# Blocks of 512 tokens: a new order of the first four attention groups and their loads, head transposes and g's low part moved forward

## The chip, the cores and the metric

The kernel runs on one core of one Trainium2 chip. The metric is the device time of one execution in microseconds; the median of several runs counts. A core has a matrix engine (TensorE, in the rows PE, its weight loads PEld), a vector engine (VectorE, DVE), an activation engine (ScalarE, ACT), GpSimd (POOL), and SyncE (SP), whose queue issues nearly all DMA transfers of this kernel. Each engine works through its own instructions in their order and waits on semaphores for the others.

## The reference

Three stages in float32, one after the other, on 3072 tokens (4 batches of 768) of 512 numbers (8 heads of 64):

```python
for c in range(nc):                       # chunks of 32 queries
    k_full = concat([mem_k, k[c_start-16 : c_end+8]])   # 8 memory keys, at most 56 others
    scores = scale * matmul(q_c, k_full.T)
    a = exp(scores - max(scores)); a = a / (sum(a) + 1e-9)
    out[c_start:c_end] = matmul(a, v_full)
x = out as (3072, 512)
h = x @ w_in                              # 512 x 2048, given as 64-bit floats
g = where(h > 0, h, exp(min(h, 0)) - 1)
x = g @ w_out                             # 2048 x 512
a = x @ w1; b = x @ w2                    # 512 x 1024 each
return ((a * b) @ w3) @ w_out2
```

## The kernel before

**Precision.** Each factor of a large product is split into a high and a low part (both in a 32-bit matmul type), and three products hi*hi, hi*lo, lo*hi are summed (`mm3`, lines 131 to 133). The weights of the middle stage lie in memory as 64-bit floats; each 128-wide piece (a job, 512 KB) is loaded by SP (`raw_cols` L147, `raw_rows` L155) and turned into two 32-bit parts by ScalarE and VectorE.

**The feed.** `Feed` runs these jobs as a pipeline: one call of `step` does the high part of job i-2 (ScalarE, L179), the low part of job i-3 (VectorE, L182), the merge of job i-1 and the rebase of job i (ScalarE, L166). A job that `by_act` selects gets one more ScalarE step (`top`, L188) and one merge on VectorE (`merge`, L192); another takes two VectorE steps (`shift` L170 and `low` L174). `load` issues the transfers of the jobs ahead, at most six beyond the one at hand. Jobs 0 to 31 alternate between columns of w_in and rows of w_out: 0, 1, 2 and 4 are w_in 0 to 3, 3 and 5 are w_out 0 and 1, 6 is w_in 4, and so on.

**Attention.** The tokens go in 24 groups of 128 (six to a batch). The steps of a group G: `load_qk` (SP: L296, L297), `load_v` (SP: L306, L310, L312; five or nine transfers), `at_first` for the first group of a batch (TensorE transposes of 8 keys and 8 memory keys, L326, copied by ScalarE to `front` and `memo`), `at_turn` (TensorE transposes of q and k, L333 and L335; six ScalarE copies), `at_scores` (L357), `at_max` (VectorE L374, L375; exponential on ScalarE L376), `at_sum` (VectorE L382 to L385), `at_norm` (L394), `at_flip` (a VectorE transpose, L405, which writes pT), `at_values` (TensorE L416), and `at_out`, which splits the result into the high part (ScalarE L127) and the low part (VectorE L128) of `xhl`, the input of the middle stage. Groups 1 and 2 have buffers and PSUM banks of their own (`pair`); group 0 and all from 3 on share one pair of banks (`banks`).

**Order of the work.** All is written out by hand; no scheduler changes it. Groups 0 to 3, which fill block 0, run in the order of the string `START`: a letter for a step and a number for the group (u first, t turn, s scores, m max, z sum, n norm, p flip, v values, o out, k load of q and k, w load of v), and `f` for one step of the feed. Behind it comes the middle stage, six blocks of 512 tokens with 16 feature tiles each. For a feature tile n: `mm_h` (12 products of x with w_in), the exponential on ScalarE (`elu_exp`, L582, L583), the max on VectorE (`elu_max`, L588), g's high part (`elu_hi`, ScalarE L592) and low part (`elu_lo`, VectorE L596), and `mm_x` (12 products of g with w_out, two tiles later). The other groups are dealt out between these: `pace` gives each step of `chain` a slot, two slots to a feature tile and eight to a group; `at_first` has -0.5, so it runs right behind the previous group's `at_out` at 7.2. In the first two tiles of a block (`first`) the function `x()` with `mm_x` and one `at_step` runs ahead of `mm_h`. The last stage is not touched by the change.

The lines of the loop in which g's low part stands:

```python
if first:
    x()
if n < NH:
    if j == 0:
        feed.until(due[f])
    mm_h(n)
...
if FF1 < n < NH:
    elu_lo(n - 1)
if not first:
    x()
```

## Time and profile before

| what | value |
|---|---|
| runs (us) | 1090.22, 1090.37, 1092.13; median 1090.37 |
| profiled execution (us) | 1091.64, its span 1089.9 |
| TensorE busy | 1039.5 us, 95% |
| VectorE busy | 569.1 us, 52% |
| ScalarE busy | 456.6 us, 42% |
| DMA | 199.17 MB, mean 183 GB/s |

The profile is one execution with the start and length of each instruction. Busy times are added per engine; an engine that is always busy sets the time, and where it is idle a row in square brackets says for how long and what ended the wait. In the rows an arrow `out<-in` names the tiles that an instruction writes and reads, and `x4` means that four of the same kind are merged in one row. A float32 matmul other than those of `mm3` shows as two records.

### The profile page before, as it was taken

The page shows a single profiled execution, that of the slowest core. Times are in us where ns is not written, and L with a number is a line of the kernel's source. Part 1 is how long each engine was busy: PE and PEld are TensorE (multiplying, and loading weights), DVE is VectorE, ACT ScalarE, POOL GpSimd, SP SyncE. Part 2 cuts the span into 40 slices and gives each one's busy share as a digit, 9 for nine tenths or more (in the row PEclk, how much of TensorE's full clock was granted, in tenths as well). Part 3 has the DMA queues.
Part 4 walks back from the last instruction along what each step waited for, and adds up shares of the span by engine and source line. Part 5 has one row for each costly group of instructions (what it writes and reads, how often), then busy time and mean ns, then how long its engine had stood idle before and what let it go on. Part 6 is the DMA issues. An engine that isn't in the chain of part 4 may idle for free.

```text
span 1089.9 us, 19197 instructions
## 1 busy us (share of the span) xinstructions
PE 1039.5 (95%) x7760; PEld 888.9 (82%) x7760; DVE 569.1 (52%) x993; ACT 456.6 (42%) x884; POOL 1.7 (0%) x16
## 2 busy tenths in 40 slices
PE   4489999999999999999999999999999999999998
PEld 3367887887888787878887888789999999999997
DVE  4678856656666565757654234144443544443333
ACT  3477756554555454545554333022232232222222
POOL 0000000000000000000000000000000000000000
PEclk9889999999999999999999999999999999999999
DMA  8777846755766575648544846455466466555521
GB/s 179 186 221 203 245 123 178 234 181 167 211 221 197 175 213 163 218 155 251 161 155 146 289 136 203 138 180 163 154 208 227 155 205 230 159 172 183 184 86 58
DMA packets 178340, 199.17 MB, mean 183 GB/s; under 512 B 101964, under 2 KB 142924, under 8 KB 178252
## 3 DMA queue, kind: packets, MB, share of 16 engines
q1 hardware_dynamic: 177212, 197.69, 58.6%
q8 instruction: 61, 1.00, 0.4%
q10 hardware_dynamic: 1040, 0.26, 0.1%
q14 instruction: 27, 0.22, 0.1%
HBM read 154.93 MB, written 42.99 MB: 182 GB/s over the span
## 4 chain that ended last, share of the span: by engine, by line
PE 91%; ACT 3%; DVE 2%; DMA 2%; SPq 1%; issue 0%; ACTq 0%; DVEq 0%
PE bank L131 20%; PE bank L132 19%; PE bank L133 19%; PE bank L710 7%; PE bank L711 7%; PE bank L709 7%; PE banks L416 2%; PE banks L133 2%; PE banks L132 2%; PE banks L131 2%; PE banks L357 1%; PE banks L333 1%; PE banks L335 1%; DMA vw<-in_v_dram 1%; PE banks L451 1%; DMA qn<-in_q_dram 1%
## 5 line engine op out<-in xcount | busy, mean ns | idle before, releaser
L131 PE MATMUL bank<-xhl,w 128*128 128x512 f32 x384 | 156.2, 407 | 1.0 <-ACT xhl L127 0.7
L132 PE MATMUL bank<-g,w 128*128 128x512 f32 x384 | 150.6, 392 | 3.6 <-DVE g L596 3.6
L131 PE MATMUL bank<-g,w 128*128 128x512 f32 x384 | 153.2, 399 | 0.0
L132 PE MATMUL bank<-xhl,w 128*128 128x512 f32 x384 | 152.0, 396 | 0.0
L133 PE MATMUL bank<-xhl,w 128*128 128x512 f32 x384 | 152.0, 396 | 0.0
L133 PE MATMUL bank<-g,w 128*128 128x512 f32 x384 | 150.1, 391 | 0.0
L582 ACT ACTIVATE eg<-bank 128x512 f32<-128x512 f32 x96 | 57.3, 597 | 121.2 <-PE bank L133 121.1
L588 DVE SCALAR_TENSOR_TENSOR eg<-eg,bank 128x512 f32<-128x512 f32 x96 | 65.6, 683 | 75.9 <-ACT eg L583 75.7
L483 DVE TENSOR_TENSOR e<-bank,e 128x384 f32<-128x384 f32 x64 | 35.7, 557 | 119.2 <-PE bank L711 119.2
L132 PEld LDWEIGHTS bank<-g,w 128*128 128x128 f32 x384 | 72.2, 188 | 19.5 <-DVE g L596 5.6
L131 PEld LDWEIGHTS bank<-xhl,w 128*128 128x128 f32 x384 | 73.3, 191 | 16.7 <-ACT xhl L127 0.9
L133 PEld LDWEIGHTS bank<-xhl,w 128*128 128x128 f32 x384 | 73.4, 191 | 15.9
L132 PEld LDWEIGHTS bank<-xhl,w 128*128 128x128 f32 x384 | 73.4, 191 | 14.8 <-DVE xhl L128 0.4
L131 PEld LDWEIGHTS bank<-g,w 128*128 128x128 f32 x384 | 72.2, 188 | 15.8 <-ACT g L592 0.2
L133 PEld LDWEIGHTS bank<-g,w 128*128 128x128 f32 x384 | 72.1, 188 | 15.1
L710 PE MATMUL bank<-xd,w 128*128 128x384 f32 x224 | 75.9, 339 | 0.0
L592 ACT CAST g<-eg 128x512 fp32r<-128x512 f32 x96 | 59.6, 621 | 35.4 <-DVE eg L588 35.1
L596 DVE TENSOR_TENSOR g<-eg,g 128x512 fp32r<-128x512 f32 x96 | 65.7, 684 | 14.8 <-ACT g L592 14.5
L483 DVE TENSOR_TENSOR e<-bank,eg 128x384 f32<-128x384 f32 x64 | 35.6, 557 | 58.8 <-PE bank L711 58.8
L711 PE MATMUL bank<-xd,w 128*128 128x384 f32 x192 | 64.8, 337 | 0.0
L709 PE MATMUL bank<-xd,w 128*128 128x384 f32 x192 | 64.2, 335 | 0.0
L583 ACT ACTIVATE eg<-eg 128x512 f32<-128x512 f32 x96 | 60.7, 632 | 3.1
(159 smaller groups left out, 1849.5 us busy)
## 6 DMA issues: line engine op xcount, KB each, us to landing
w<-wqd SPq DMA_DIRECT2D x96, 512.0 KB
raw<-in_moe_w_dram SPq DMA_DIRECT2D x32, 512.0 KB
w<-shd SPq DMA_DIRECT2D x30, 512.0 KB
wqd<-st SPq DMA_DIRECT2D x24, 512.0 KB
raw<-in_moe_w_out_dram SPq DMA_DIRECT2D x22, 512.0 KB
w3d<-st SPq DMA_DIRECT2D x16, 512.0 KB
w<-w3d SPq DMA_DIRECT2D x16, 512.0 KB
w<-wqd SPq DMA_DIRECT2D x32, 256.0 KB
```

Source lines behind the costliest of these rows:

```text
L131: mm(o, lhsT=w_hi, rhs=x_hi, start=start, stop=False)
L132: mm(o, lhsT=w_hi, rhs=x_lo, start=False, stop=False)
L133: mm(o, lhsT=w_lo, rhs=x_hi, start=False, stop=stop)
L483: nc.vector.tensor_tensor(out=o, in0=a, in1=b, op=op)
L582: nc.scalar.activation(e, h_t[n], AF.Relu, scale=-1.0)
L583: nc.scalar.activation(e, e, AF.Exp, scale=-1.0)
L588: nc.vector.scalar_tensor_tensor(out=e, in0=e, scalar=-1.0, in1=h_t.pop(n), op0=ALU.add, op1=ALU.max)
L592: nc.scalar.copy(g_t[n][:, 0, :], eg_t[n])
L596: nc.vector.tensor_tensor(out=g[:, 1, :], in0=eg_t.pop(n), in1=g[:, 0, :].bitcast(F32), op=ALU.subtract)
L709: mm(o, lhsT=args[0], rhs=args[2], start=start and i == 0, stop=False, skip_group_check=more)
L710: mm(o, lhsT=args[0], rhs=args[3], start=False, stop=False, skip_group_check=more)
L711: mm(o, lhsT=args[1], rhs=args[2], start=False, stop=i == 1, skip_group_check=more)
```

## The change

- `START` has a new order, and new words `l3`, `l4`, `l6`, which allow the feed to load so many jobs and issue those loads there. The feed's new field `cap` holds this limit: 2 ahead of the string, and all jobs behind it. The loads ahead of the string are q and k of groups 0, 1, 2, then v of group 0, then two weight jobs.
- `by_act` selects three of four later jobs in place of one of two.
- `at_first` of group 0 writes to another bank. From group 6 on it is called as `first_next` at slot 4.6 of the group before.
- `at_turn` copies `front` and `memo` first, and for groups 0 and 1 the copy of q goes to VectorE.
- A first ScalarE copy from the cleared `front` to `memo` is new.
- `elu_lo(n - 1)` stands ahead of `x()` in the first two tiles of a block, from the second tile of block 1 on.

```diff
@@ -69,7 +69,7 @@
     LATER = (11, 12, 13, 14, 15, 27, 28, 29, 30, 31)
     SHARED = {2: 24, 3: 25, 4: 26}
 
-    START = "u0 t0 k3 f s0 t1 f m0 s1 z0 n0 m1 p0 t2 v0 w3 s2 z1 n1 p1 m2 o0 t3 v1 s3 z2 n2 p2 f o1 v2 m3 f o2 z3 n3 p3 k4 v3 w4 f o3 f"
+    START = "u0 t0 w1 k3 l3 w2 l4 t1 s0 m0 s1 m1 t2 f z0 n0 p0 s2 f m2 v0 w3 l6 z1 n1 o0 p1 t3 f z2 n2 s3 v1 p2 m3 k4 f o1 v2 z3 n3 o2 p3 f v3 w4 f o3"
     SCALE = 1.0 / float(D) ** 0.5
     assert GQ == P and KEYS == 64 and KT == 4 and HP == 4 and DM == 512
 
@@ -206,15 +206,15 @@
 
 
         def __init__(self, jobs):
-            self.jobs, self.at, self.loaded = jobs, 0, 0
+            self.jobs, self.at, self.loaded, self.cap = jobs, 0, 0, 0
 
         def load(self, n):
-            while self.loaded < min(len(self.jobs), n):
+            while self.loaded < min(self.cap, n):
                 self.jobs[self.loaded].fetch()
                 self.loaded += 1
 
         def by_act(self, i):
-            return i < 6 or i % 2 == 1
+            return i < 6 or i % 4 != 2
 
         def do(self, i, *ops):
             if 0 <= i < len(self.jobs):
@@ -321,7 +321,7 @@
         if G % GPS:
             return
         n = RIGHT + NM
-        pk = bank(G, 1, n)
+        pk = bank(1 if G == 0 else G, 1, n)
         for hp in range(HP):
             nc.tensor.transpose(pk[:, hp, :], pair(head, hp), ident[:n, :n])
         nc.scalar.copy(front[:, :, 0, LEFT:FRONT], pk[:, :, 0:RIGHT])
@@ -334,13 +334,13 @@
         for hp in range(HP):
             nc.tensor.transpose(pk[:, hp, :], pair(kn, hp), ident)
         qT = at_tile(G, at_p, [P, HP, GQ], "qT", "qp")
-        nc.scalar.copy(qT, pq)
         kT = at_tile(G, at_p, [P, HP, NCG, KEYS], "kT", "ke")
         blocks = pk.rearrange("p a (c k) -> p a c k", k=CH)
+        nc.scalar.copy(kT[:, :, 0:1, 0:FRONT], front)
+        nc.scalar.copy(kT[:, :, :, WIN:KEYS], memo.to_broadcast([P, HP, NCG, NM]))
+        copy_on("v" if G < 2 else "a", qT, pq)
         nc.scalar.copy(kT[:, :, :, FRONT:WIN], blocks)
         nc.scalar.copy(kT[:, :, 1:NCG, 0:FRONT], blocks[:, :, 0:NCG - 1, CH - FRONT:CH])
-        nc.scalar.copy(kT[:, :, 0:1, 0:FRONT], front)
-        nc.scalar.copy(kT[:, :, :, WIN:KEYS], memo.to_broadcast([P, HP, NCG, NM]))
         if G % GPS < GPS - 1:
             nc.scalar.copy(front[:, :, 0, :], blocks[:, :, NCG - 1, CH - FRONT:CH])
         qT_t[G], kT_t[G] = qT, kT
@@ -503,9 +503,10 @@
 
 
     load_next = lambda G: load_qk(G + 1)
+    first_next = lambda G: at_first(G + 1) if G + 1 < NG else None
     load_next_v = lambda G: load_v(G + 1)
-    chain = (at_first, at_turn, load_next, at_scores, at_max, at_sum, at_norm, at_flip, at_values, at_out, load_next_v)
-    pace = (-0.5, 0, 0, 2, 3, 4, 5, 6, 7, 7.2, 7.5)
+    chain = (at_turn, load_next, at_scores, at_max, at_sum, first_next, at_norm, at_flip, at_values, at_out, load_next_v)
+    pace = (0, 0, 2, 3, 4, 4.6, 5, 6, 7, 7.2, 7.5)
     slots = {}
 
     def put(at, fn, arg):
@@ -790,28 +791,29 @@
         first_late = min(due[i] for i in LATER)
         feed = Feed(jobs)
 
+        nc.gpsimd.memset(front, 0.0)
         load_qk(0)
+        nc.scalar.copy(memo, front[:, :, :, 0:NM])
         make_identity(nc, ident)
-        nc.gpsimd.memset(front, 0.0)
         nc.gpsimd.memset(vw[0:LEFT, 0], 0.0)
         for c in range(NCG):
             for s in range(2):
                 nc.gpsimd.memset(odd[c * CH:(c + 1) * CH, s], float(c % 2 == s))
-        feed.load(1)
         load_qk(1)
+        load_qk(2)
+        load_v(0)
+        feed.cap = 2
         feed.load(2)
-        load_v(0)
-        load_qk(2)
-        load_v(1)
-        feed.load(3)
-        load_v(2)
-        feed.load(5)
         one = dict(t=at_turn, u=at_first, s=at_scores, m=at_max, z=at_sum, n=at_norm, p=at_flip, v=at_values, o=at_out, k=load_qk, w=load_v)
         for what in START.split():
             if what == "f":
                 feed.step()
+            elif what[0] == "l":
+                feed.cap = int(what[1])
+                feed.load(feed.cap)
             else:
                 one[what[0]](int(what[1]))
+        feed.cap = len(jobs)
         early_psum.close()
         psum_x = ctx.enter_context(tc.tile_pool(name="psum_x", bufs=1, space=PSUM))
         for i in range(KT):
@@ -851,6 +853,8 @@
                     elu_max(n)
                 at_step()
 
+            if first and FF1 < n < NH:
+                elu_lo(n - 1)
             if first:
                 x()
             if n < NH:
@@ -869,7 +873,7 @@
             at_step()
             if spread:
                 elu_exp(n)
-            if FF1 < n < NH:
+            if FF1 < n < NH and not first:
                 elu_lo(n - 1)
             if not first:
                 x()
```

The first instructions of SP's queue, of before and of after; `kn`, `qn` and `vw` are the tiles of k, q and v, `raw` a weight tile.

```order
 L293 DMA head<-in_k_dram 8x8x64
 L294 DMA head<-in_mem_k_dram 8x8x64
 L297 DMA kn<-in_k_dram 128x8x64
-L147 DMA raw<-in_moe_w_in_dram 128x4x256
-L296 DMA qn<-in_q_dram 128x8x64
-L297 DMA kn<-in_k_dram 128x8x64
-L147 DMA raw<-in_moe_w_in_dram 128x4x256
+L296 DMA qn<-in_q_dram 128x8x64
+L297 DMA kn<-in_k_dram 128x8x64
+L296 DMA qn<-in_q_dram 128x8x64
+L297 DMA kn<-in_k_dram 128x8x64
```

Behind group 0's k, the q and k of groups 1 and 2 now follow without a weight tile between them.

SP's queue around the end of `START`, before (the v load in the middle of it is group 4's; `more` is a weight tile in a spare buffer, `shd` a copy of weights that is stored):

```order
43 L147 DMA raw<-in_moe_w_in_dram 128x4x256
44 L306 DMA vw<-in_v_dram 128x8x64
45 L310 DMA vw<-in_v_dram 24x8x64 x4
46 L155 DMA raw<-in_moe_w_out_dram 128x1024
47 L147 DMA raw<-in_moe_w_in_dram 128x4x256
48 L296 DMA qn<-in_q_dram 128x8x64
49 L297 DMA kn<-in_k_dram 128x8x64
50 L306 DMA vw<-in_v_dram 128x8x64
51 L310 DMA vw<-in_v_dram 24x8x64 x4
52 L155 DMA raw<-in_moe_w_out_dram 128x1024
53 L235 DMA shd_164<-w_77 128x1024
54 L147 DMA more<-in_moe_w_in_dram 128x4x256
```

The same place after; the v load in the first two rows is group 4's, and the first weight row is job 6:

```order
46 L306 DMA vw<-in_v_dram 128x8x64
47 L310 DMA vw<-in_v_dram 24x8x64 x4
48 L235 DMA shd_164<-w_77 128x1024
49 L147 DMA raw<-in_moe_w_in_dram 128x4x256
50 L155 DMA raw<-in_moe_w_out_dram 128x1024
51 L147 DMA raw<-in_moe_w_in_dram 128x4x256
52 L155 DMA raw<-in_moe_w_out_dram 128x1024
53 L147 DMA more<-in_moe_w_in_dram 128x4x256
54 L155 DMA more<-in_moe_w_out_dram 128x1024
```

Three weight tiles (jobs 6 to 8) that stood ahead of group 4's v load now stand behind it and behind the store.

VectorE at the beginning of block 3, before; `g<-eg,g` is the low part of g, `eg<-eg,bank` the max, `st` tiles are weights of the last stage and, in the last two rows, the block's output:

```order
291 L588 SCALAR_TENSOR_TENSOR eg<-eg,bank_96 128x512
292 L182 TENSOR_TENSOR st<-st 128x512
293 L483 TENSOR_TENSOR st<-f 128x256
294 L483 TENSOR_TENSOR st<-st,f 128x256
295 L483 TENSOR_TENSOR st<-f,st 128x256
296 L182 TENSOR_TENSOR st<-st 128x512
297 L596 TENSOR_TENSOR g<-eg,g 128x512
298 L588 SCALAR_TENSOR_TENSOR eg<-eg,bank_95 128x512
299 L124 COPY st<-bank_722 128x512
300 L124 COPY st<-bank_724 128x512
```

And after:

```order
287 L589 SCALAR_TENSOR_TENSOR eg<-eg,bank_96 128x512
288 L597 TENSOR_TENSOR g<-eg,g 128x512
289 L182 TENSOR_TENSOR st<-st 128x512
290 L483 TENSOR_TENSOR st<-f 128x256
291 L483 TENSOR_TENSOR st<-st,f 128x256
292 L483 TENSOR_TENSOR st<-f,st 128x256
293 L182 TENSOR_TENSOR st<-st 128x512
294 L589 SCALAR_TENSOR_TENSOR eg<-eg,bank_95 128x512
295 L597 TENSOR_TENSOR g<-eg,g 128x512
296 L124 COPY st<-bank_713 128x512
297 L124 COPY st<-bank_715 128x512
```

The low part of g now follows directly on the max that it needs, ahead of the weight steps and of the output copies.

## Rows read from the trace of the kernel before

**Rows 1.** The page, first part: busy time, share and instructions of each engine.
```profile
PE 1039.5 (95%) x7760; PEld 888.9 (82%) x7760; DVE 569.1 (52%) x993; ACT 456.6 (42%) x884; POOL 1.7 (0%) x16
```

**Rows 2.** Stretches: from:to, length, busy (instructions) of each engine, granted clock, DMA share, GB/s.
```profile
0.00:51.29 51.29, 20.37 (x549) 16.93 (x549) 25.62 (x47) 20.57 (x49) 1.73 (x16) 0.93 0.80 184
51.29:73.30 22.01, 21.70 (x144) 16.94 (x144) 15.98 (x29) 16.84 (x33) 0.00 (x0) 0.86 0.93 284
...
79.40:100.00 20.60, 20.60 (x151) 16.82 (x151) 16.20 (x31) 16.32 (x32) 0.00 (x0) 0.95 0.80 202
```

**Rows 3.** Waits of TensorE: line, releaser, us in total, times, longest.
```profile
PE banks L416 <- DVE pT L405: 10.8, 2, 6.6
PE banks L333 <- DMA qn<-in_q_dram: 7.0, 1, 7.0
...
PE banks L326 <- DVE xhl L128: 4.4, 3, 1.5
...
PE bank L132 <- DVE g L596: 3.6, 5, 0.8
```

**Rows 4.** Timeline of TensorE up to the first product: start, length, instruction, idle before.
```profile
6.80 1.12 PE L333 MATMUL banks<-ident,qn 128*128 128x128 f32 x4 [1.71 <-ACT memo L328]
...
15.79 1.18 PE L357 MATMUL pair<-kT,qT 64*32 64x64 f32 x64 [1.97 <-ACT front L345]
...
33.01 1.09 PE L333 MATMUL banks<-ident,qn 128*128 128x128 f32 x4 [7.03 <-DMA qn<-in_q_dram]
...
48.57 2.01 PE L416 MATMUL banks<-pT,vw 64*64 64x64 f32 x64 [6.58 <-DVE pT L405]
51.29 0.79 PE L131 MATMUL bank<-xhl,w 128*128 128x512 f32 x1 [0.70 <-ACT xhl L127]
```

**Rows 5.** Timeline of VectorE, the middle of group 3.
```profile
39.71 0.68 DVE L374 TENSOR_REDUCE mx<-banks 128x8 f32<-128x512 f32 x1
40.42 0.69 DVE L375 TENSOR_TENSOR e<-banks,mx 128x512 f32<-128x512 f32 x1
41.03 0.68 DVE L182 TENSOR_TENSOR w<-f,w 128x512 fp32r<-128x512 f32 x1
...
44.58 0.68 DVE L382 TENSOR_REDUCE sm<-e 128x8 f32<-128x512 f32 x1
...
45.94 1.29 DVE L394 TENSOR_TENSOR e<-e,rc 128x512 f32<-128x512 f32 x2
47.27 1.25 DVE L405 STREAM_TRANSPOSE pT<-e 128x1024 f32<-128x1024 f32 x1
```

**Rows 6.** Timeline of ScalarE around the first product.
```profile
50.65 0.58 ACT L127 CAST xhl<-banks 128x512 fp32r<-128x512 f32 x1 [5.08 <-PE banks L416]
...
53.71 0.68 ACT L166 ACTIVATE f<-raw 128x512 f32<-128x512 f32 x1
58.33 0.59 ACT L337 COPY qT<-banks 128x512 f32<-128x512 f32 x1 [3.93 <-PE banks L335]
```

**Rows 7.** Timeline of SP's queue: q of group 3, weight jobs, v transfers.
```profile
27.00 0.43 SPq L296 DMA_DIRECT2D qn<-in_q_dram  x1
...
31.62 0.39 SPq L147 DMA_DIRECT2D raw<-in_moe_w_in_dram  x1
...
42.38 0.39 SPq L147 DMA_DIRECT2D raw<-in_moe_w_in_dram  x1
...
50.86 2.20 SPq L310 DMA_DIRECT2D vw<-in_v_dram  x4
```

**Rows 8.** Timeline of TensorE, values of group 4.
```profile
77.61 1.82 PE L416 MATMUL banks<-pT,vw 64*64 64x64 f32 x64 [4.25 <-DVE pT L405]
```

**Rows 9.** Timeline of TensorE, head transposes of group 6.
```profile
106.94 0.42 PE L326 MATMUL banks<-ident,head 16*128 16x16 f32 x4 [1.46 <-DVE xhl L128]
```

**Rows 10.** Timeline of VectorE and TensorE, low part of g in block 3.
```profile
371.97 0.69 DVE L596 TENSOR_TENSOR g<-eg,g 128x512 fp32r<-128x512 f32 x1
...
372.71 0.50 PE L132 MATMUL bank<-g,w 128*128 128x512 f32 x1 [0.84 <-DVE g L596]
```

## The prediction

> **What bounds the kernel now.** I read the page first: TensorE is busy for 95% of the span [rows 1], so only its idle time, 1089.9 - 1039.5 = 50.4 us, is there to be won. The table by stretch says where that lies [rows 2]: up to the first product (matmul L131 at 51.29 us, called T0 here) TensorE is busy for 20.37 of 51.29 us, so 30.9 us of idle stand there, and the other 19.5 us are spread over the 1038.6 us behind it. The list of waits then names the pieces [rows 3]: in the front, the value products L416 waiting for the transposed weights pT, and the transposes L333 of group 3 waiting for its q; later, 4.4 us in three waits of the head transposes L326 for a VectorE subtraction, and 3.6 us in five waits of L132 for g's low part. A fourth piece, 4.25 us at 77.61 [rows 8], is the larger remainder of "L416 <- pT". Two limits follow: before T0 a chain of loads and of VectorE and ScalarE steps; after T0 TensorE itself, with short holes.
>
> **The front.** Groups 0 to 3 go through first (head), turn, scores, max, sum, norm, flip, values, out. The kernel before ran them nearly one after another, because group 3's q is issued only at 27.00 us, behind weight tiles, and its transposes start at 33.01 [rows 7, 4]. Now q and k of groups 1 and 2 are issued right behind group 0's, group 3's right behind the second v, and weight tiles 0 and 1 behind the first v. No operation on the data is added or removed; two q copies go from ScalarE to VectorE. I work out the new T0 step by step.
>
> Turn 0 began at 6.80 after 1.71 us of waiting for the copy of the memory keys [rows 4]. That copy no longer stands ahead of it (another bank is used, and the table load of ScalarE is done early by a copy of zeros); what remains is the arrival of q0 and k0, which is nowhere later than 6.80. I take 6.0. Two turns are four sets of transposes at 1.09 us: 10.4. The scores of group 0, 1.18 us: 11.6 [rows 4].
>
> From there VectorE is the engine with the most to do. One group costs it, start to start in [rows 5]: max 0.71, subtraction 0.61, the sum and its small steps 45.94 - 44.58 = 1.36, norm 47.27 - 45.94 = 1.33, flip 1.25; together 5.26, four groups 21.0. In between stand seven 512-wide operations at 0.6 each (three low parts of x, three merges of weight jobs, one low part of a weight): 4.2. So the last flip could end at 11.6 + 25.2 = 36.8. Waits come on top: the merges of jobs 0 and 1 and the low part of group 1 stand behind ScalarE steps that need a raw tile, and raw 0 is now issued behind the first v instead of as SP's fourth transfer. The nearest landing in the trace is group 3's q, 27.00 to 33.01 = 6.0 us [rows 7, 4]. If both places wait to the full it is about 3 us each; if the tiles are in time, nothing. I take 2.3, so the flip ends at 39.1. The values of group 3 last 2.08 (48.57 to 50.65), so they end at 41.2 [rows 4, 6].
>
> Here the new order has a price: the feed step that stood behind "o3" now stands ahead of it. ScalarE must do the high part of job 3, which waits for VectorE's next two operations (39.1 + 1.2 = 40.3), and a rebase and a top, none over 0.68 [rows 6]; at 0.6 each that is 42.1, and then the high part of x, 0.64 from start to T0 (50.65 to 51.29). T0 is about 42.7 against 51.29: **8.6 us gained**. With no waits it is 40.4 (10.9 gained); with 6 us of them 46.4 (4.9), and 1.5 us more if a v tile is late by a quarter of that landing time: 3.4 gained.
>
> The q copies on VectorE: the order of the changed program makes ScalarE's k copy wait for VectorE's q copy, both reading one PSUM tile. No row of before shows two engines reading such a tile side by side, so the bounds are 0 and 0.6 us per turn (one copy, [rows 6]); I have counted them one after the other, and for group 0 they lie under turn 1. The Trainium skill (PSUM — Partial Sum Buffer, section "PSUM bank collisions raise a hardware error") says that two engines collide only on the same bank, reads included, and that other banks may be read together; q and k lie in the two banks of the tile. By that rule the wait is not needed and T0 could be 0.6 earlier; by the order it is there.
>
> **Behind T0.** The cap on the feed moves transfers, too. Before, weight jobs 6, 7 and 8 are issued between 31.62 and 42.38 [rows 7] (the first and the last of three). Now jobs 6 to 11 are issued only behind the v load of group 4, which waits for the values of group 3, and behind a 512 KB store. Four v transfers take 2.20 us to issue [rows 7], six transfers so 3.3: job 6 is issued at 41.2 + 3.3 = 44.5 and lands, at 6.0 us, at 50.5 = T0 + 7.8. ScalarE is in order, and its rebase of job 6 stands ahead of group 4's q and k copies and of the first exponential. It ran at 53.71 without a wait; then ScalarE stood idle for 3.93 us until the turn of group 4 was ready at 58.33 = T0 + 7.04 [rows 6]. This idle time hides the new wait up to T0 + 6.4. What is left over is 7.8 + 0.68 - 7.04 = 1.4 us, and it goes straight into the first exponential and TensorE: **1.4 lost** (0 if it lands in 4.6 us, 3 if in 7.6). Of the 144 matmuls between 51.29 and 73.30 [rows 2] 72 are scores and transposes and 72 are products, six weight tiles' worth; six tiles of 0.52 MB take 11 us of these 22 at that row's 284 GB/s, so the next jobs are in time.
>
> Every second even-numbered job from 8 on is merged with ScalarE's help: VectorE saves one operation, ScalarE gets one of at most 0.68 us. Between 51.29 and 73.30 ScalarE is busy 16.8 us and VectorE 16.0 of 22.0 [rows 2]; neither has much the better of it, so I take nothing, and leave the 4.25 us hole before the values of group 4 [rows 8] as it is (bounds: gone, or 1 us longer).
>
> **Head transposes.** Before, they follow group G-1's output directly and wait until VectorE has read the bank: 1.46 us at 106.94 [rows 9], three times, 4.4 in all [rows 3]. Now they stand two slots earlier, behind a whole product and after the max step has emptied the bank. The work itself (0.42 us) stays. The next user of the bank, the turn of group G, comes one product later than the waiting L326 did, and no L333 waits for that subtraction in [rows 3]. **4.4 gained** (3.0 if one of the three remains).
>
> **g's low part.** At a block's begin VectorE did, between the two parts of g, other work of the attention and of the weight jobs; L132 waited 0.84 us at 372.71 for the subtraction begun at 371.97 [rows 10]. Now that subtraction stands directly behind the previous block's last max. Five blocks have such a wait; for block 1 the old branch stays, so four go: 4 x 0.84 = **3.3 gained**, at worst 2.5 because VectorE now waits for ScalarE's high part in front of other work.
>
> **Sum.** -8.6 + 1.4 - 4.4 - 3.3 = -14.9 us. The profiled execution took 1091.64 us (span 1089.9), 1.3 above the median of 1090.37; from it the sum gives 1076.7, from the median 1075.5. I forecast 1076.1.
>
> **Rivals.**
> 1. *The front's gain is taken back by late weights.* The lead of three tiles (1.57 MB) is gone; at the 202 GB/s of 79.4 to 100 us [rows 2] their transfer takes 7.8 us. If all of it shows, the time is about 1084. For it: DMA shares of 0.93 and 0.80 there. Against it: the 11 of 22 us above. Chance 0.10.
> 2. *The front does not get faster.* The six feed steps wait in order for tiles that land later than I think, and T0 stays at 51. Then only heads and g count: 1091.64 - 7.7 = 1084, or 1083 from the median. For it: the first weight tile now stands behind nine v transfers. Against it: before T0 VectorE is busy for half the time only, 25.6 of 51.3 us [rows 2]. Chance 0.08.
> 3. *The later waits come back under other names*, L333 or L131 waiting for the same subtractions: -8.6 + 1.4 = -7.2 gives 1084, or 1083 from the median. Chance 0.06.
> 4. *Slower: block 0 is fed from hand to mouth.* If from T0 + 7 on each weight tile lands after it is due, TensorE stops once per feature tile of block 0. A stop like that at 77.61 costs 4.25 us, and the row of 51.29 to 73.30, with a granted clock of 0.86, shows that products right behind a pause run in part at the lower of the two levels (1.2 instead of 2.4 GHz): another 1 us. Three such stops (15.8 us) use up the gain of 14.9; from the fourth on it is slower, and with four or five the time is about 1096. For it: the shares of DMA. Against it: the wait at 77.61 is for VectorE, and no wait for a weight's transfer stands among the large ones [rows 3]. Chance 0.05.
>
> **Chances.** The forecast has 0.71. Its own range is 1069.5 to 1081.5 (front 3.4 to 10.9 gained; job 6 0 to 3 lost; heads and g 5.5 to 7.7; the hole 1 longer to 4.25 shorter; not all at one end). Rivals 1 to 3 lie at 1083 to 1084; to leave out no more than 2 in 10 the whole range goes from 1069.5 to 1083.5. A change of 0.2% is about 2.2 us, what a measurement of this kernel can tell from none; all cases but the fourth are beyond it: faster 0.92, same 0.03, slower 0.05.
>
> **What would show it.** Right: the first L131 near 43 us, DVE nearly without gaps from 12 us to the last flip, no L326 in the list of waits behind T0, one wait of L132 for g of some 0.2 us left. Wrong: T0 beyond 47; ScalarE idle for a raw tile of more than 3 us at the rebase of job 6; new waits of TensorE for weights in the stretch up to 100 us; granted clock under 0.86 there.

## The result, and the profile after

| kernel | median (us) | runs | span of the profiled execution |
|---|---|---|---|
| before | 1091.21 | 1090.22 to 1092.13 (4) | 1089.9 |
| after | 1073.24 | 1072.24 to 1074.06 (4) | 1072.3 |

The ratio is 0.9835, 95% interval 0.9818 to 0.9852: 18.0 us faster, against a forecast of 1076.1 in a range of 1069.5 to 1083.5. The same kernel, run again later, gave 1074.28, a ratio of 0.9848 (label a2_again below), so the gain is 16.6 to 18.0 us.

The page's first part, after. TensorE's busy time is 3.0 us less than in [rows 1]; most of the gain is idle time that has gone.

```profile
PE 1036.5 (97%) x7760; PEld 886.5 (83%) x7760; DVE 567.7 (53%) x989; ACT 459.3 (43%) x889; POOL 1.7 (0%) x16
```

The stretches after, columns as in [rows 2]: up to T0, the 22.01 us behind it, and on to 76 us.

```profile
0.00:41.94 41.94, 18.93 (x549) 15.90 (x549) 28.28 (x51) 22.15 (x51) 1.74 (x16) 0.74 0.87 189
41.94:63.95 22.01, 20.89 (x143) 16.44 (x144) 13.63 (x25) 14.85 (x30) 0.00 (x0) 0.87 1.02 306
63.95:76.00 12.05, 7.29 (x82) 5.76 (x81) 11.04 (x18) 8.33 (x17) 0.00 (x0) 0.72 0.57 168
```

TensorE is idle for 23.0 us ahead of T0 instead of 30.9, but for 1.1 and 4.8 us in the two stretches behind it, where the granted clock, too, is lower than full. The waits of TensorE after (line, releaser, total, times, longest), to hold against [rows 3]:

```profile
PE banks L416 <- DVE pT L405: 9.1, 2, 4.8
...
PE banks L333 <- DVE pT L405: 4.2, 1, 4.2
...
PE bank L131 <- ACT xhl L127: 1.4, 1, 1.4
...
PE bank L131 <- DVE eg L589: 1.0, 1, 1.0
```

Of the list of before, the waits of L326 for VectorE and of L132 for g are gone altogether. The timeline of TensorE after (start, length, instruction, idle before it), to hold against [rows 4, 8]:

```profile
5.22 1.11 PE L333 MATMUL banks<-ident,qn 128*128 128x128 f32 x4
...
38.52 2.01 PE L416 MATMUL banks<-pT,vw 64*64 64x64 f32 x64 [4.38 <-DVE pT L405]
41.94 0.79 PE L131 MATMUL bank<-xhl,w 128*128 128x512 f32 x1 [1.40 <-ACT xhl L127]
...
53.33 0.50 PE L131 MATMUL bank<-xhl,w 128*128 128x512 f32 x1 [1.02 <-DVE eg L589]
...
69.26 2.01 PE L416 MATMUL banks<-pT,vw 64*64 64x64 f32 x64 [4.76 <-DVE pT L405]
```

T0 is 41.94. Behind it stand a wait for VectorE's max at 53.33 (1.02 us; 0.30 before) and the hole ahead of the values of group 4, 4.76 us [rows 8: 4.25].

Where the 17.6 us between the two spans come from is read by following the same places through both traces: the first transpose (L333) of a group's turn, and the first L131 at T0 and in the last stage. Each column is one execution.

| place | start before | start after | gained so far | what lies between |
|---|---|---|---|---|
| T0 | 51.29 | 41.94 | 9.35 | the front |
| turn of group 5 | 83.23 | 75.73 | 7.50 | -1.85: block 0 behind T0 |
| turn of group 6 | 110.16 | 101.37 | 8.79 | +1.29: wait of L326 |
| turn of group 11 | 237.33 | 228.22 | 9.11 | +0.3: block 1, among it the wait of L132 of 0.23 |
| turn of group 12 | 264.70 | 254.31 | 10.39 | +1.28: wait of L326 |
| turn of group 13 | 291.36 | 279.85 | 11.51 | +1.12: wait of L132 of 0.84 |
| turn of group 17 | 394.56 | 381.98 | 12.58 | +1.17 ahead of it: wait of L132 |
| turn of group 18 | 423.54 | 408.07 | 15.47 | +2.89: wait of L326 and what follows |
| turn of group 21 | 501.29 | 484.67 | 16.62 | +1.17 ahead of it: wait of L132 |
| last stage (first wait for w) | 691.31 | 673.67 | 17.64 | +1.09: wait of L132 |

So the front brought 9.35, block 0 took back 1.85, the three places of the head transposes brought 5.46 and the five of g's low part 4.9 (a drift of 0.2 the other way is spread between). The largest step, from the turn of group 17 to that of group 18, before and then after:

```profile
394.56 0.60 PE L333 MATMUL banks<-ident,qn 128*128 128x128 f32 x4
...
423.54 0.60 PE L333 MATMUL banks<-ident,qn 128*128 128x128 f32 x4
```

```profile
381.98 0.60 PE L333 MATMUL banks<-ident,qn 128*128 128x128 f32 x4
...
408.07 0.60 PE L333 MATMUL banks<-ident,qn 128*128 128x128 f32 x4
```

One row of the places emptied, TensorE after: the head transposes of group 6, which waited 1.46 us in [rows 9], now run without a gap.

```profile
88.67 0.42 PE L326 MATMUL banks<-ident,head 16*128 16x16 f32 x4
```

### The profile page after: what moved, and what is told of

Same layout as the page of the kernel before. It is cut to its first block, busy times and chain, and to the rows that moved or that the text cites. A ratio compares the mean times of both kernels' runs of the same rounds, so it can differ in the third digit from the quotient of the medians.

```text
span 1072.3 us, 19201 instructions
## 1 busy us (share of the span) xinstructions
PE 1036.5 (97%) x7760; PEld 886.5 (83%) x7760; DVE 567.7 (53%) x989; ACT 459.3 (43%) x889; POOL 1.7 (0%) x16
## 4 chain that ended last, share of the span: by engine, by line
PE 93%; DMA 2%; DVE 2%; ACT 1%; SPq 1%; issue 0%; DVEq 0%; ACTq 0%
PE bank L131 20%; PE bank L132 20%; PE bank L133 20%; PE bank L711 7%; PE bank L712 7%; PE bank L710 7%; PE banks L416 2%; PE banks L133 2%; PE banks L132 2%; PE banks L131 2%; DMA vw<-in_v_dram 2%; PE banks L357 1%; PE banks L335 1%; PE banks L333 1%; PE banks L451 1%; DMA raw<-in_moe_w_in_dram 1%
## 5 line engine op out<-in xcount | busy, mean ns | idle before, releaser
L131 PE MATMUL bank<-xhl,w 128*128 128x512 f32 x384 | 155.7, 406 | 2.4 <-ACT xhl L127 1.4
L131 PE MATMUL bank<-g,w 128*128 128x512 f32 x384 | 153.6, 400 | 0.0
L132 PE MATMUL bank<-xhl,w 128*128 128x512 f32 x384 | 151.6, 395 | 0.0
L132 PE MATMUL bank<-g,w 128*128 128x512 f32 x384 | 150.2, 391 | 0.0
L131 PEld LDWEIGHTS bank<-xhl,w 128*128 128x128 f32 x384 | 73.0, 190 | 18.4 <-ACT xhl L127 1.6
L131 PEld LDWEIGHTS bank<-g,w 128*128 128x128 f32 x384 | 72.1, 188 | 15.9
L132 PEld LDWEIGHTS bank<-xhl,w 128*128 128x128 f32 x384 | 73.2, 191 | 14.6 <-DVE xhl L128 0.4
L132 PEld LDWEIGHTS bank<-g,w 128*128 128x128 f32 x384 | 72.2, 188 | 14.2 <-DVE g L597 0.3
```

What stands on the lines that cost most here:

```text
L131: mm(o, lhsT=w_hi, rhs=x_hi, start=start, stop=False)
L132: mm(o, lhsT=w_hi, rhs=x_lo, start=False, stop=False)
```

## Experiments

Each is an edit of the changed kernel; ratios are to the kernel before, run beside it. A difference to the changed kernel is taken from the two ratios, times 1091, against both of its measurements (0.9835 and 0.9848), so a range is given. My theory was: each of the three parts acts by itself where the prediction put it, and the loss in block 0 comes from job 6's late issue. The rivals stand with each expectation.

**Head transposes in their old place.** The old `chain` and `pace` (`at_first` first, at -0.5).

> The changed kernel with the head transposes back at their old place, right behind the previous group's output (slot -0.5); all else as changed. Theory: the three waits of L326 for the subtraction L128 return, 1.46 us each, and behind one or more of them TensorE runs for some products at the lower clock level; in the trace of before, behind the wait at 418.76, the products stood 0.43 instead of 0.23 us apart until 422.8 (granted clock 0.50 between 420 and 422), 1.6 us. So 4.4 to 6.0 us slower than the changed kernel (1073.2): 1077.6 to 1079.2. Rival (only the listed waits count): 4.4 us, and no row behind an L326 shows a clock under 1. Second rival (the wait had another cause, and the gain of that size came from the front): under 1.5 us.

Measured: 1080.12 us (ratio 0.9896, 0.9881 to 0.9910), 5.2 to 6.7 us slower than the changed kernel. TensorE's timeline shows the three waits back, 1.46 us each as in [rows 9]:

```profile
99.55 0.42 PE L326 MATMUL banks<-ident,head 16*128 16x16 f32 x4 [1.46 <-DVE xhl L128]
...
255.19 0.42 PE L326 MATMUL banks<-ident,head 16*128 16x16 f32 x4 [1.46 <-DVE xhl L128]
...
410.07 0.42 PE L326 MATMUL banks<-ident,head 16*128 16x16 f32 x4 [1.46 <-DVE xhl L128]
```

The 3.5 us behind each of them, same kernel (columns as in the stretches above; the clock stands third from the end):

```profile
99.97:103.50 3.53, 3.53 (x11) 2.77 (x12) 3.05 (x6) 2.26 (x7) 0.00 (x0) 0.64 0.85 177
255.60:259.00 3.40, 3.40 (x19) 2.85 (x19) 2.68 (x6) 1.78 (x6) 0.00 (x0) 1.00 0.41 90
410.50:414.00 3.50, 3.50 (x11) 2.74 (x12) 3.25 (x7) 1.40 (x4) 0.00 (x0) 0.65 0.39 88
```

From group to group this trace falls behind that of the changed kernel by 2.82 us at the first wait, 1.28 at the second and 2.76 at the third (group 5 to 6: 75.73 to 101.37 after, 75.87 to 104.33 here), 6.9 in all, and by nothing elsewhere up to the last group. So the waits were not hidden by anything later (that rival falls), and together they cost more than their own 4.4 us: behind two of three TensorE works for some 3 us at the lower level. The one with full clock behind it cost 1.28, less than its 1.46.

**g's low part in its old place.** The `elu_lo` call ahead of `x()` removed, the old one restored.

> The changed kernel with g's low part back behind the other VectorE work in the first two feature tiles of a block. Theory: the five waits of L132 for the low part return, 0.24 us in block 1 and 0.84 in the four others, 3.6 in all; since the row before such a wait starts 1.23 us ahead instead of 0.23, each costs about 1.0 and the step costs 4.2 us: 1077.4. Rival: only the listed 3.6 us, 1076.8. Second rival (the wait is only traded for one of VectorE elsewhere): nothing, 1073.2.

Measured: 1077.39 us (ratio 0.9873, 0.9858 to 0.9888), 2.7 to 4.1 us slower. TensorE's waits of this kernel between 100 and 600 us hold four of L132, three of 0.47 and one of 0.82:

```profile
PE bank L132 <- DVE g L597: 2.2, 4, 0.8
```

The changed kernel has none there. Each wait of 0.47 puts the next group's values (L416) back by 0.73 against the trace of the unaltered changed kernel (a2_again: 250.93 to 276.46 us there, 250.92 to 277.19 here): wait plus 0.26. So the step is worth something (the second rival falls), but the expected 4.2 lies at the upper end of the range and the first rival's 3.6 within it. Three of the waits are little more than half of those in [rows 10], and the one in block 1 did not come back at all: other parts of the change act on them too. Which ones was not tried.

**The old front with the rest of the change.** Old `START`, and the old list of loads in front of it (cap set to all jobs).

> The changed kernel with the old order string and the old loads ahead of it (weight tiles 0 and 1 early, no cap); the later parts (heads, low part of g, three of four jobs by ScalarE, q copies) as changed. Theory: the first product moves back from 41.9 to about 51 us, and what is lost behind it in block 0 (1.9 us, from 9.4 gained at the first product to 7.5 at the turn of group 5) does not occur: 1073.2 + 7.5 = 1080.7. Rival (the q copies on VectorE, the early table load and the order of the six copies in a turn carry part of the front's gain): the first product at 48 to 50 and 1077 to 1079.

Measured: 1079.64 us (ratio 0.9892, 0.9878 to 0.9907), 4.8 to 6.2 us slower, less than the 7.5 expected. Its TensorE:

```profile
50.15 0.79 PE L131 MATMUL bank<-xhl,w 128*128 128x512 f32 x1 [0.71 <-ACT xhl L127]
```

T0 is 8.2 us behind the changed kernel's, but at the values of group 4 only 5.9 (75.13 against 69.26): 2.3 of them are lost again between T0 and those values, where the old front has job 6 in time. T0 is also 1.1 us earlier than before (51.29), so the rival is right to that extent: something in the rest of the change, not told apart here, carries 1.1 us of the front's gain.

Put back one at a time, the three parts cost 12.8 to 17.0 us together, where the whole change brought 16.6 to 18.0. The theory that each acts by itself holds only roughly.

**The new loads with nearly the old order of steps.**

```diff
-START = "u0 t0 w1 k3 l3 w2 l4 t1 s0 m0 s1 m1 t2 f z0 n0 p0 s2 f m2 v0 w3 l6 z1 ...
+START = "u0 t0 w1 k3 l3 w2 l4 s0 t1 f m0 s1 z0 n0 m1 p0 t2 v0 w3 l6 f s2 z1 n1 p1 m2 o0 t3 k4 ...
```

> The changed kernel's order of the loads with nearly the old order of the computing steps of groups 0 to 3 (turn, scores, feed step and max of a group ahead of the next group's). Theory A (the loads carry the gain, because group 3's q was what TensorE waited 7 us for): the first product at 42 to 44 us, 1073 to 1075. Theory B (the order of the steps on VectorE and ScalarE carries it, since feed steps now stand ahead of attention steps whose weight tile lands later): the first product at 46 to 50, 1077 to 1081.

Measured: 1081.03 us (ratio 0.9904, 0.9888 to 0.9921). T0, in TensorE's timeline:

```profile
48.58 0.79 PE L131 MATMUL bank<-xhl,w 128*128 128x512 f32 x1 [0.71 <-ACT xhl L127]
```

Against the old front with the rest of the change (e3), the new loads alone move T0 by 1.6 us (50.15 - 48.58), and the kernel ends no earlier (1.4 us later, in overlapping ranges). The other 6 us of T0, down to the 42.6 that is the mean of the profiles below, come with the order of the steps: theory B. The new order with the old loads was not tried.

**The changed kernel again**, as a control for the next ones.

> The changed kernel once more, unaltered, as the measure for the runs beside it. 1072 to 1075; first product between 41.5 and 43.5 us (the profiled executions of two kernels with the same front showed 41.94 and 43.2).

Measured: 1074.28 us (1073.10 to 1076.02; ratio 0.9848, 0.9834 to 0.9861). Its T0 is 43.01, 1.07 later than in the first trace. ScalarE's timeline shows why: the rebase of job 3 (the first w_out tile) waits for its transfer. The row after first, then that of the control:

```profile
31.75 0.66 ACT L166 ACTIVATE f<-raw 128x512 f32<-128x512 f32 x1 [0.17 <-DMA raw<-in_moe_w_out_dram]
```

```profile
32.83 0.66 ACT L166 ACTIVATE f<-raw 128x512 f32<-128x512 f32 x1 [1.66 <-DMA raw<-in_moe_w_out_dram]
```

In all seven profiles that have this front unaltered from there on (after, a2, e1, e2, e4, e8, e11) T0 comes 10.18 or 10.19 us behind that rebase, which in each of them waits for its transfer: 31.50 and 41.69 are the earliest pair, 33.06 and 43.24 the latest. The mean T0 of the seven is 42.6.

**Weight jobs 6 to 8 ahead of the values of group 1.**

```diff
-... p2 m3 k4 f o1 v2 z3 ...
+... p2 m3 k4 l9 f o1 v2 z3 ...
```

> The changed kernel with a word l9 behind k4 in the order string: weight jobs 6, 7 and 8 are issued at about 35 us instead of behind the v load of group 4 (43.1). Theory: ScalarE's wait of 6.56 us for job 6 (to 48.96) goes; the copies of group 4 then start when its turn ends (48.4), the first exponential about 0.9 us earlier, the wait of the third h product for it (1.02) shrinks to 0.1 to 0.3: 0.7 to 1.0 us faster than the changed kernel. Rival 1 (the job's lateness costs nothing, since VectorE's queue sets the values of group 4): same within 0.3. Rival 2 (three tiles more in flight delay job 4 or the v of group 3): first product 1 us later or more, slower.

Measured: 1071.70 us (ratio 0.9824, 0.9810 to 0.9837), 2.6 us under the control (1.2 against the first measurement of the changed kernel). ScalarE's rebase of job 6, after and here:

```profile
48.96 0.66 ACT L166 ACTIVATE f<-raw 128x512 f32<-128x512 f32 x1 [6.56 <-DMA raw<-in_moe_w_in_dram]
```

```profile
42.07 0.67 ACT L166 ACTIVATE f<-raw 128x512 f32<-128x512 f32 x1
```

It no longer waits, the first exponential comes 7.90 us behind T0 (49.60 - 41.70) instead of 9.32 (51.26 - 41.94), and the 1.02 us wait at h2, the third h product, is gone. The hole of group 4's values stays (4.73 us). From T0 to the turn of group 5 it takes 31.32 us here, 33.79 after and 33.29 in the control. So job 6 did cost 1.4 us at that exponential, and 1.2 to 2.6 in the end (the times' intervals overlap; the trace carries the claim), more than the 0.7 to 1.0 that I expected here.

**The last feed step behind group 3's output** (`v3 w4 f o3` to `v3 w4 o3 f`).

> The changed kernel with the last feed step of the order string back behind o3. Theory: in the changed kernel TensorE waits 1.40 us for the high part of x, 0.7 of it because ScalarE does the step first; with it behind, the first product comes 0.7 us earlier, and ScalarE has idle time later for the step: 0.7 us faster. Rival: the step's weight work is then late for the second and third product, and nothing is gained (0 to 0.5 slower).

Measured: 1073.50 us (ratio 0.9838, 0.9825 to 0.9852), 0.8 us under the control and 0.3 above the first measurement of the changed kernel, within the spread of all. In the trace the wait of the first L131 for the high part of x falls from 1.40 to 0.70 us. The 0.7 us can be read at T0, not in the time.

**Values of group 4 one slot later.**

```diff
 for at, fn in zip(pace, chain):
+    if G == GPB and fn in (at_values, at_out, load_next_v) or G == GPB + 1 and fn in (at_turn, load_next):
+        at += 1
```

> The changed kernel with values, output and v load of group 4 one slot later (behind the fifth h product instead of ahead of it), and the turn and load of group 5 one slot later too. Theory: the hole of 4.76 us before these values is partly filled by 2.7 us of product; about 2 us of hole stay, and the clock does not fall behind it (in the changed kernel the products from 71.2 to 74.8 stand 0.43 us apart, about 1.7 us lost): 3 to 4.5 us faster than the changed kernel, 1069 to 1070. Rival (VectorE's queue limits all of this stretch): the hole moves behind, to the next x product or to the scores of group 5, and at most 1 us is won.

Measured: 1069.72 us (1069.46 to 1069.91; ratio 0.9805, 0.9791 to 0.9818), 4.6 us under the control (3.3 against the first measurement of the changed kernel). TensorE at those values:

```profile
69.50 1.30 PE L416 MATMUL banks<-pT,vw 64*64 64x64 f32 x64 [1.11 <-DVE pT L405]
```

VectorE's flip ends no earlier than in the changed kernel (68.20 + 1.24 us against 67.96 + 1.24); TensorE only has products to do meanwhile. The stretches from the hole on, of the changed kernel and then of this one:

```profile
69.30:75.73 6.43, 6.43 (x76) 5.33 (x77) 5.42 (x10) 3.40 (x8) 0.00 (x0) 0.57 0.61 149
```

```profile
68.00:76.00 8.00, 6.45 (x90) 4.98 (x89) 7.51 (x13) 7.10 (x14) 0.00 (x0) 1.00 0.47 140
```

The granted clock is 1.00 instead of 0.57. Against that first trace the hole of 4.76 us and the slow products behind it are gone, less what now waits (0.54 for eg, 1.11 for pT, 0.44 at the turn of group 5); from T0 to the turn of group 6 it is 55.51 us here and 59.44 there. The rival, at most 1 us won, falls.

The hole is not a fixed price, though. In the control it is 3.24 us, and the clock has fallen already ahead of it (0.76 from 52 to 59 us, at waits of 0.86 and 1.03):

```profile
70.70 1.42 PE L416 MATMUL banks<-pT,vw 64*64 64x64 f32 x64 [3.24 <-DVE pT L405]
```

Of the ten profiles of the changed kernel and its variants that have these values in their old slot, four show that earlier fall and a hole of 3.15 to 3.24 (a2, e2, e5, e7); the other six have a hole of 4.25 to 4.76.

**Both, and all three together.**

> Both edits that were faster alone: weight jobs 6 to 8 issued ahead of the values of group 1 (alone 2.6 us under the control of its call) and group 4's values, output and next v one slot later, with group 5's turn one slot later (alone 4.6 under it). Theory A (two different losses: the first takes away the 1.02 us wait for eg at h2 and job 6's landing, the second the hole before the values of group 4): they add, near 1067 us, with the first product near 42, no wait for eg at 53 and no wait over 1 us behind it up to 100 us. Theory B (one loss: VectorE late by job 6, paid once wherever TensorE first meets it): they do not add, 1069 to 1070, as the second alone.

> As e9_jobs_and_values, and the last feed step of the order behind group 3's output, which alone gave 0.8 us under the control. Theory A (the feed step on ScalarE delays the high part of x by the 0.7 us seen there): 0.7 under e9_jobs_and_values, so near 1066.5, and the first product waits 0.7 instead of 1.4 us for the high part. Theory B (what it gives at the first product is taken back at the next weight): equal to e9_jobs_and_values within 0.3.

Measured: e9 1068.48 us (ratio 0.9788, 0.9775 to 0.9801), e10 1067.70 us (1067.09 to 1068.47; ratio 0.9783, 0.9769 to 0.9796). From 0.9805 (e8 alone) e9 goes down by 0.0017, 1.9 us, where theory A has 2.6 and B 0; the intervals overlap, so the times alone don't decide. The traces do: the wait of 1.03 at h2 is gone, and the values of group 4 start 26.46 us behind T0 (69.48 - 43.02) instead of 27.81 (69.50 - 41.69), 1.35 sooner. They add, if not to the full; one wait over 1 us is left ahead of those values (1.15), which theory A did not have. What e10 adds, 0.0005, is within the intervals. TensorE of e10:

```profile
41.84 0.79 PE L131 MATMUL bank<-xhl,w 128*128 128x512 f32 x1 [0.70 <-ACT xhl L127]
...
67.25 1.28 PE L416 MATMUL banks<-pT,vw 64*64 64x64 f32 x64 [1.15 <-DVE pT L405]
```

This version, 6 to 7 us under the changed kernel and 23 under the one before, is the fastest that was run.

**q of groups 0 and 1 in tiles of its own.**

```diff
+        if G < 2:
+            pq = PS[KT + G].rearrange("p (a b) -> p a b", b=GQ)
```

> The changed kernel with the transposed q of groups 0 and 1 in two other PSUM tiles (banks that stand free until the first product), so that VectorE's copy of q and ScalarE's copy of k read different tiles and nothing in the program orders them. Theory A (other banks may be read by two engines together): the k copy of group 0 starts within 0.1 us of the q copy instead of 0.72 behind it, both keep their lengths of 0.69 and 0.59, and the scores of group 1 start some 0.6 earlier (10.5 instead of 11.1). The maximum of group 0 still starts near 10.6, because its scores stand behind turn 1 on TensorE; VectorE sets the time from there, so the first product moves by 0.3 us or less and the kernel stays at 1073 to 1075. Theory B (two engines reading PSUM get in each other's way): copies longer by a fifth or more, or still one behind the other. Theory C (the 0.6 us of the prediction reach the first product): 1073.6 beside a control at 1074.2, and all three groups behind it 0.6 earlier.

Measured: 1073.92 us (ratio 0.9838, 0.9824 to 0.9851): no difference. The timeline of the first turns (line numbers are 2 higher here):

```profile
5.68 1.11 PE L337 MATMUL banks<-ident,kn 128*128 128x128 f32 x4
5.89 0.69 DVE L124 COPY qT<-bank 128x512 f32<-128x512 f32 x1 [5.89 <-PE bank L335]
...
6.83 0.59 ACT L344 COPY kT<-banks 128x512 f32<-128x512 f32 x1 [1.30 <-PE banks L337]
...
10.37 1.18 PE L359 MATMUL pair<-kT,qT 64*32 64x64 f32 x64
...
10.74 0.69 DVE L376 TENSOR_REDUCE mx<-banks 128x8 f32<-128x512 f32 x1
```

VectorE now copies q while TensorE still writes k into another bank, and ScalarE follows as soon as k is there; the copies keep their lengths. The scores of group 1 come 0.74 earlier than after (10.37 instead of 11.11), but the max of group 0, which stands behind turn 1, does not (10.74 and 10.62), and T0 is again 10.18 behind the rebase of job 3. So theory A holds for the time; the two copies were not seen at the same instant, since k arrives 0.94 later than q.

**The old division of the merges** (`i % 4 != 2` back to `i % 2 == 1`).

> The changed kernel with the old division of the merges alone: jobs 8, 12, 16 and so on merged by VectorE without ScalarE's help. Theory A (the prediction: neither engine has the better of it): within 0.7 us of the changed kernel's 1073.2 to 1074.3. Theory B (VectorE is the one that is late between the first product and the values of group 4): one operation of 0.6 us more ahead of that flip, so that wait is 0.6 longer, and the time 0.6 to 1.2 higher, up to 1075.5; behind 100 us no wait of TensorE changes.

Measured: 1074.23 us (ratio 0.9841, 0.9828 to 0.9855): no difference, theory A. The hole of group 4's values is 4.25 us in its trace, not longer.

## Why the prediction was right, point by point

- **The front**: predicted T0 42.7, measured 41.94 once and 42.6 as the mean of seven profiles. The steps: turn 0 at 5.22 (6.0 said), max of group 0 at 10.62 (11.6), end of the last flip at 38.46 (39.1). VectorE was busy for 22.97 of the 26.46 us between 12 us and that end, so 3.5 us of gaps against the 2.3 taken. Group 3's late q, named first, does not carry the front alone: with the new loads and nearly the old steps (e5) T0 is 48.58. The place of the waits differs, too: the two raw tiles named, 0 and 1, cost ScalarE 0.29 and 1.60 us,

```profile
16.29 0.69 ACT L166 ACTIVATE f<-raw 128x512 f32<-128x512 f32 x1 [0.29 <-DMA raw<-in_moe_w_in_dram]
...
19.13 0.67 ACT L166 ACTIVATE f<-raw 128x512 f32<-128x512 f32 x1 [1.60 <-DMA raw<-in_moe_w_in_dram]
```

  while the tile by which T0 moves is that of job 3, which the prediction did not look at. SP issues it at 28.02, behind nine v transfers of group 2:

```profile
28.02 0.36 SPq L155 DMA_DIRECT2D raw<-in_moe_w_out_dram  x1
```

  VectorE's longest wait in the front stands behind ScalarE's work on that job:

```profile
33.45 0.69 DVE L128 TENSOR_TENSOR xhl<-pair,xhl 128x512 fp32r<-128x512 f32 x1 [1.93 <-ACT xhl L127]
```

  Issuing the tile earlier was not tried.
- **Behind T0**: predicted job 6 issued at 44.5, landed 7.8 us behind T0, 1.4 us lost. Measured, SP's queue:

```profile
43.13 0.42 SPq L147 DMA_DIRECT2D raw<-in_moe_w_in_dram  x1
```

  43.13 and 48.96, a landing of 5.83 us, 7.02 behind T0, and by e6 1.42 us at the first exponential: the mechanism and the size. Against before that exponential comes only 0.52 later (9.32 instead of 8.80 us behind T0), since with job 6 in time it would come 0.9 sooner (7.90 in e6), which the prediction did not count. From T0 to turn 5 the loss is 1.85 in the first trace, of which 0.53 stand at h2 (11.39 instead of 10.86 us behind T0), 0.47 more at the values of group 4 and 0.85 behind them, in products at the lower clock level. The five profiles with the same program up to there, but for e11's q copies (after, a2, e1, e2, e11), lose 0.68 to 1.85, 1.35 on the mean, beside the 1.4 said; their turn 5 stands at 75.73 to 76.60, where the prediction's terms give 76.04 (42.7 + 31.94 + 1.4). The hole "left as it is" was 3.23 to 4.76 in them.
- **Head transposes**: predicted 4.4, measured 5.46, as 1.29, 1.28 and 2.89. A wait of 1.46 us with full clock behind it cost 0.2 less than its length, so the three by themselves bring 3.9, less than predicted. The other 1.6 us come from one thing that was left out: behind the third wait of before the granted clock fell (0.66 from 418 to 423 us). It fell behind one such wait of three there and two of three in e1, so it differs from trace to trace, and what decides it was not found. (The transposes moved by 2.9 slots, from -0.5 to 4.6 of the group before, not by the two named.)
- **g's low part**: predicted 3.3 from four waits of 0.84, measured 4.9 between the two traces. Each of the four places gave 1.09 to 1.17, 4.55 together. TensorE before, around the wait of [rows 10]:

```profile
371.25 0.39 PE L133 MATMUL bank<-xhl,w 128*128 128x512 f32 x1
371.48 0.39 PE L131 MATMUL bank<-g,w 128*128 128x512 f32 x1
372.71 0.50 PE L132 MATMUL bank<-g,w 128*128 128x512 f32 x1 [0.84 <-DVE g L596]
373.05 0.40 PE L133 MATMUL bank<-g,w 128*128 128x512 f32 x1
```

  The product ahead of the wait starts 1.23 us before L132, where its neighbours stand 0.23 apart: the interval lost is 1.00, not the 0.84 in brackets, and the next follows after 0.34 instead of 0.23. The other 0.3 belong to block 1, whose wait of 0.23 was said to stay and went too. It is absent from e2 as well, where g's low part has its old place, so another part of the change removed it. With the rest of the change in place the step is worth 2.7 to 4.1 us (e2); that 3.3 lies in this range is partly luck, since the waits there are of 0.47 and not 0.84.
- **q copies**: by the order the k copy waits for the q copy, and so it was (ScalarE's row after, first turn, with VectorE's 0.69 ahead of it):

```profile
7.23 0.69 DVE L124 COPY qT<-banks 128x512 f32<-128x512 f32 x1 [7.23 <-PE banks L335]
7.95 0.59 ACT L342 COPY kT<-banks 128x512 f32<-128x512 f32 x1 [1.94 <-DVE qT L124]
```

  The Trainium skill (PSUM — Partial Sum Buffer, section "PSUM bank collisions raise a hardware error") lets two engines read different banks at once. The changed kernel shows it at a block's end, where the copies of the sums read different banks, ScalarE's pair until 158.89 and VectorE's from 158.55 on; the trace agrees, with VectorE's copy at 0.68 us where one that reads alone takes 0.69 (7.23 above).

```profile
157.82 1.07 ACT L122 COPY st<-bank 128x512 f32<-128x512 f32 x2
```

```profile
158.55 0.68 DVE L124 COPY st<-bank 128x512 f32<-128x512 f32 x1
```

  The 0.6 us that the prediction put on this wait at T0 do not get there: e11, without the wait, has the same T0 behind the rebase of job 3.
- **Merges**: nothing said, nothing measured (e4).
- **Rivals**: none came. Rival 1 (late weights) and 4 (hand to mouth) would show TensorE waiting for weights up to 100 us: only job 6 was late, through the exponential. Rival 2 needed T0 at 51, which only e3, with the old front, shows (50.15). Rival 3 fell with e1 and e2: with the old places the waits of L326 come back at 1.46 and those of L132 at 0.47 to 0.82, and the changed kernel has no L333 or L131 waiting for the same subtractions. Rival 4's time does not follow from its own terms: four or five stops of 5.25 us on top of 1076.1 are 1097 to 1102, not 1096.
- **Two of the signs set as wrong did appear** and were badly set. ScalarE idle for more than 3 us ahead of job 6 (6.56): the prediction's own landing at T0 + 7.8 implied that, and what counts is how far the idle time outlasts turn 4. A clock under 0.86 up to 100 us: 0.87 in the first 22 us, but 0.72 from 63.95 to 76, the stretch of the hole. One of the signs set as right did not appear: no wait of L132 of 0.2 us was left.

The total was 2.9 us short. Between the two traces it is 17.64 against 14.9 us: 1.6 from the lower clock behind one head transpose, 1.2 from g's four waits priced by the length in brackets, 0.7 from the first trace's early T0 and 0.3 from block 1's wait; the other way, 0.5 from head waits that cost less than their length, 0.45 from block 0 and the drift of 0.2. So the mechanism was right in each part, and the two waits were mis-sized in both directions.

## What to carry to other kernels

Price a wait of the bounding engine by the distance between the starts of the instructions on both sides, less what it is elsewhere (0.84 in brackets cost 1.09 to 1.17 here, 1.46 only 1.28), and look at the granted clock of the few microseconds behind it. A wait that is "left as it is" is worth asking whether the waiting engine has other work that could stand ahead of it: one slot of delay was worth 3.3 to 4.6 us here, with the late engine no faster. In a start-up chain, look for the transfer that the end moves with from run to run; it need not be the longest wait in any one trace.

## What the runs showed of the hardware

- Equal waits of TensorE, 1.46 us at L326, were followed by full clock (2.4 GHz) in three of six cases (before twice, e1 once) and, in the other three, by a mean of 0.64 to 0.66 over 3.5 to 5 us, that is, mostly by the lower level (1.2 GHz). A place cost 1.28 or 1.29 us in the first kind and 2.76 to 2.89 in the second. What decides between them was not found; the place at 255 to 262 us stayed at full clock in both kernels. The 4.76 us hole was followed by 6.43 us at 0.57; the same hole of 4.73 us in e1 by 5.37 us at 0.71.
- One transfer of 512 KB, issued at the same point of the program (27.19 to 28.53 us), reached ScalarE at 31.50 to 33.06 us in seven profiles, 3.73 to 5.26 us behind its issue, and the first product moved with it to 0.01 us. That is a spread of 1.5 us in the front of one kernel; by group 5 the traces of e1 and after, 1.3 apart at T0, were 0.14 apart again. Nearly all of that (1.10 us) was made up behind group 4's values, where the granted clock was 0.71 in e1 and 0.57 after.
